# Attention and two mixing layers on one core: the last 64 tokens of q and k in one bank, and another rule for when the weights' parts are moved

## The chip, the cores and the metric

The kernel runs on one core of a Trainium2 chip. The metric is device time in microseconds of one execution, from the launch to the last output in memory. Below, block names and times refer to the profiled execution of the kernel before unless it is said otherwise.

## The reference

Three stages in fp32. The first is attention with exponential features, the second a gated channel mix, the third a convolution with a gate. Cut to what is computed:

```python
# q, k, v: (8, 8, 576, 64); w_phi: (64, 128)
proj = einsum('bhsd,df->bhsf', x, w_phi)
proj = proj - max(abs(proj), axis=-1)
phi(x) = concat([exp(proj), exp(-proj)])          # 256 features
kv = phi(k)^T v ; z = sum(phi(k)) ; out = phi(q) kv / (phi(q) z + 1e-6)
# channel mix on (8, 576, 512): xk, xr are mixtures of x and x one token back
k = relu(xk @ w_k) ; r = sigmoid(xr @ w_r) ; x2 = r * (k*k @ w_v)
# conv stage
h = relu(x2 @ w_in) ; out = (h * sigmoid(conv3(h, conv_w))) @ w_out
```

## The kernel before

**Attention.** Two heads of a batch are a pair; there are 32 pairs, and block(Pi) does the work around pair Pi. The 576 tokens are four tiles of 128 and a rest of 64. Tile `rqk` holds both heads of a pair: head h has the partitions 64h to 64h+63 (its 64 dimensions), and the columns are q of the first 512 tokens, then the last 64 tokens of q, then the last 64 of k, then the first 512 of k. A block runs on three pairs at once: it transposes the features of q of pair Pi (`turn`, `turn_end`: tiles `pt`, `pr`, features `qf` on ScalarE), projects the rest of q and k and the k of pair Pi + 2 (`front`: `rows_last` into `p1`, which the trace calls `p`, and `rows4` into `pk`), projects q of pair Pi + 1 (`pq`), sums kv of Pi + 1 (`pkv`), and computes the results of pair Pi (`pn`). VectorE centres each projection (`centre`: a reduction `mx` and a subtraction into `t`) and normalises the results (`rd`, `xn`); ScalarE makes the features of k (`kp` and, for the last 64 tokens, `kr`). The finished rows `xn` are transposed by `column` (`px`) and copied to `xT`.

**The last 64 tokens.** `rows_last` multiplies the 128 columns (64 of q, 64 of k) of each head with w_phi: two matmuls on 64 rows of the array, one for each head, each into a bank of its own. The tokens come out as partitions, 0 to 63 those of q, 64 to 127 those of k. `features` reads the k half for `kr` (four instructions on 64 partitions), `turn_end` transposes the q half, one transpose for each head.

**The channel mix.** u counts 16 half batches of 288 tokens. A u has 8 steps `psk`, and twice two steps `psr` and two `psv` (which take two credits each). Where one batch's four pairs are through, its u can run. `feed` gives steps behind block(Pi): none up to block 3, then 6, 6, 7 and 9 for blocks 4 to 7 (`SR`), 10 from block 8 on. u = 0 multiplies fp32 weights (`wkl`, `wrh`, `wvl`) directly, two instructions a matmul; later u use a high and a low half (three matmuls).

**The weights' parts.** w_k, w_r and w_v come as 64-bit floats and are turned into fp32 on the chip, 20 parts of 512 columns: 1 to 8 of w_k, 9 and 10 of w_r, 11 to 14 of w_v, 15 and 16 of w_r, 17 to 20 of w_v. `step` is a generator for one part with three stretches: SP loads `raw` (512 KB, three buffers); ScalarE reads it into `h`; VectorE finishes `h` with four instructions and SP stores it as a part (256 KB) into the weight tile. `tick()` sends one load off and finishes the part whose load went off two ticks earlier; `pre()` does ScalarE's read ahead of that tick. So the load of part k + 3, which needs the buffer of part k, stands on SP's queue behind the store of part k. Who calls tick: block(Pi) twice in blocks −1 to 6; `extras` at numbered places behind blocks 4, 5 and 6 (`WAT`); and `want(n)`, called by every step of a u with the number n of the part that it needs: it ticks until n + 2 parts (`AHEAD`) are done.

**What sets the order.** TensorE's instructions stand in the order in which the code above issues them, block by block, with the steps of the channel mix between blocks. For the other engines a scheduler orders the instructions at build time; on the chip each engine then takes its own in that order. `psm` is a ring of three PSUM banks (`p`, `pq` and the channel mix), `psa` one of five; from block 5 on a block takes from `psa` in turn `px`, `pt`, `pt`, `pr`, `pk`, `pk`, `pq`, `pkv`, `pn`, `pn`, so that the second `pk` takes the bank of `px`, the first `pq` that of the first `pt`.

Of the kernel before, what the change touches and what calls it, by code (L numbers as in the profile page):

```python
# [27 lines left out]

MS, SLOW, SR = 4, 8, {4: 6, 5: 6, 6: 7, 7: 9}

WAT = {4: (4, 10), 5: (3, 7, 11), 6: (3, 5, 7, 9)}
DS0 = 10
AHEAD = 2
HS = S // 2
V1 = D + 1

# [6 lines left out]
def fused_kernel(ctx: ExitStack, tc: tile.TileContext, qk, va, wphi, ones2, mu, wk, wv, wr, win, wout, cw, out):  # L43
# [113 lines left out]
    with ExitStack() as p1:  # L157
# [103 lines left out]
                T.matmul(o, x[r, j * P:j * P + P], wp0[r, h * FT:h * FT + FT], start=True, stop=True)  # L261

        def rows_last(Pi):
            ps = [psm.tile([P, 512], F32, tag="mm", name="p1") for _ in range(2)]
            ps = [p_[:, :FT].rearrange("p (a n) -> p a n", a=1) for p_ in ps]
            rows(Pi, [(ps[h][:, 0], h, 4) for h in range(2)])
            t = pool.tile([P, 1, 2, FT], F32, tag="t1", bufs=2, name="t")
            for h in range(2):
                centre(ps[h], t[:, :, h])
            ts[Pi] = [t]  # L270

        def rows4(Pi, j0, nm):
# [22 lines left out]
        def features(Pi, tk):  # L295
            kp = kps_[Pi] = []
            for h in range(2):
                k_ = pool.tile([P, 4, 2, FT], F32, tag="kp", bufs=2, name="kp")
                A.activation(k_[:, :, 0], tk[h], AF.Exp)
                A.activation(k_[:, :, 1], tk[h], AF.Exp, scale=-1.0)  # L300
                kp.append(k_)

            k_ = pool.tile([P, 2, FT], F32, tag="kr", bufs=1, name="kr")
            for h in range(2):
                r = slice(64 * h, 64 * h + 64)
                A.activation(k_[r, 0], ts[Pi][0][64:, 0, h], AF.Exp)
                A.activation(k_[r, 1], ts[Pi][0][64:, 0, h], AF.Exp, scale=-1.0)
            kp.append(k_)

        def sums4(Pi):  # L310
# [42 lines left out]
            return qf, t1  # L353

        def turn_end(qf, t1, pr):
            for h in range(2):
                T.transpose(pr[:, P + h * P:2 * P + h * P], t1[:, 0, h], ident)
            for h in range(2):
                for c in range(2):
                    A.activation(qf[h][:, c, 512:], pr[:, P + h * P:P + h * P + 64], AF.Exp, scale=1.0 - 2 * c)  # L360

        def results(Pi, qf):

# [24 lines left out]
        def block(Pi):  # L388

            nq, nk = Pi + 1 < B * NP, Pi + 2 < B * NP  # L390
            if 0 <= Pi < B * NP - 3:
                load(Pi + 3)
            if Pi >= 0:
                if Pi > MS:
                    x = column(Pi - 1)
                qf, t1 = turn(Pi)
                pr = psa.tile([P, 512], F32, tag="at", name="pr")
                if Pi > MS:
                    copies = column_end(*x, pr)
                turn_end(qf, t1, pr)  # L400
                if Pi > MS:
                    copies()
            pre()
            if nk:
                tk = front(Pi + 2)
            if -1 <= Pi < 7:
                tick()
            if 1 <= Pi <= MS:
                x = column(Pi - 1)
                column_end(*x, psm.tile([P, 512], F32, tag="mm", name="pr"))()  # L410
            if nq:
                ts[Pi + 1] += centre4(rows4(Pi + 1, 0, "pq"), "tq")
                del xk[Pi + 1]
                sums4(Pi + 1)
            if Pi >= 0:
                results(Pi, qf)
            pre()
            if nk:
                features(Pi + 2, tk)
                if Pi + 2 > 1:  # L420
                    load_v(Pi + 2)
            if -1 <= Pi < 7:
                tick()

        def attention(Pi):
# [39 lines left out]

        done = [0]

        def want(n):

            while ready[0] < min(n + AHEAD, 20):  # L470
                tick()
            due[0] += 1

        due = [0]
        needs = [*range(1, 9), 9, 10, 12, 14, 15, 16, 18, 20]

        def moe(u):
            b, hf = divmod(u, 2)

            def mm(ps, wh, wl, xh, xl, first, last):  # L480
                if u:
                    mm3(ps, wh, wl, xh, xl, first, last)
                else:
                    T.matmul(ps, f(wl), xh, start=first, stop=last)

            def need(n):
                want(n)
                if u:
                    split(n)

            def soon():
                if u == 0 and due[0] < len(needs) and ready[0] < min(needs[due[0]] + AHEAD, 20):
                    pre()
            o = hf * HS
            for j in range(2):
                while not mix_next(u, j):
                    yield
            xh, xl = mixed.pop((u, 0))
            k2 = []
            for fp in range(FC // 2):  # L500
                kf = tmps.tile([P, 2, HS], F32, tag="tmp", name="kf")
                for j in range(2):
                    ps = psm.tile([P, 512], F32, tag="mm", name="psk")[:, :HS]
                    fc = 2 * fp + j
                    need(fc + 1)
                    for c in range(KC):
                        w = slice(fc * DM + c * P, fc * DM + c * P + P)
                        mm(ps, wkh[:, w], wkl[:, w], xh[:, c], xl[:, c], c == 0, c == KC - 1)
                    A.activation(kf[:, j], ps, AF.Relu)
                    soon()  # L510
                    if u == 1:
                        split()
                    yield
                if u == 0:
                    kh = main.tile([P, 2, HS], F32, tag="kh", bufs=4, name="kh")
                    A.square(kh, kf)
                    k2.append((kh, kh))
                    continue
                if u == 1:
                    A.square(kf, kf)  # L520
                else:
                    V.tensor_tensor(kf, kf, kf, ALU.mult)
                kh = main.tile([P, 2, HS], F32R, tag="kh", bufs=4, name="kh")
                kl = main.tile([P, 2, HS], F32R, tag="kl", bufs=4, name="kl")
                A.copy(kh, kf)
                V.tensor_tensor(kl, kf, f(kh), ALU.subtract)
                k2.append((kh, kl))
            rh, rl = mixed.pop((u, 1))
            for mp in range(2):
                sg = main.tile([P, 2, HS], F32, tag="sg", bufs=1, name="sg")  # L530
                for j in range(2):
                    ps = psm.tile([P, 512], F32, tag="mm", name="psr")[:, :HS]
                    mc = 2 * mp + j
                    need(9 + 6 * mp + j)
                    for c in range(KC):
                        w = slice(mc * DM + c * P, mc * DM + c * P + P)
                        mm(ps, wrh[:, w], wrl[:, w], rh[:, c], rl[:, c], c == 0, c == KC - 1)
                    A.activation(sg[:, j], ps, AF.Tanh, scale=0.5)
                    soon()
                    if u == 1:  # L540
                        split()
                    yield
                mix_next(u + 1, mp)
                x2 = tmps.tile([P, 2, HS], F32, tag="tmp", name="x2")
                for j in range(2):
                    ps = psm.tile([P, 512], F32, tag="mm", name="psv")[:, :HS]
                    mc = 2 * mp + j
                    need(12 + 6 * mp + 2 * j)
                    for kc in range(FC):
                        w = slice(mc * DFF + kc * P, mc * DFF + kc * P + P)  # L550
                        kh, kl = k2[kc // 2]
                        mm(ps, wvh[:, w], wvl[:, w], kh[:, kc % 2], kl[:, kc % 2], kc == 0, kc == FC - 1)
                    if u < 2:
                        split()
                    soon()
                    yield
                    if u < 2:
                        split()
                    V.scalar_tensor_tensor(x2[:, j], sg[:, j], 1.0, ps, ALU.add, ALU.mult)
                    yield  # L560
                (SY if u else G).dma_start(x2s[b][:, 2 * mp:2 * mp + 2, o:o + HS], x2)
# [12 lines left out]
        load_v(1)  # L574

        def extras(Pi, n):
            if n in WAT.get(Pi, ()):
                tick()
            if n + 1 in WAT.get(Pi, ()):
                pre()  # L580
            if Pi == 7 and n == 14:
                taps()
            if Pi >= DS0 and dsteps and n in (3, 11):
                dsteps[0] = dsteps[0][0](), dsteps[0][1]
            if Pi >= DS0 and dsteps and n in (4, 12):
                raw, step = dsteps.pop(0)
                step(raw)
# [177 lines left out]
```

## Time and profile before

| | us |
|---|---|
| median of the runs (range) | 1225.81 (1225.13 to 1226.35) |
| the profiled execution | 1225.83 |
| its span, first to last instruction | 1224.0 |
| TensorE busy | 1202.0 (98%) |
| VectorE busy | 762.1 (62%) |
| ScalarE busy | 696.7 (57%) |

In the page's slices TensorE is at 7 to 8 tenths in the first two and at 9 from the third on, while VectorE begins at 7, 9, 8 and 9 tenths and falls to 5 to 7. The granted clock is full in every slice. Of the chain that ended last TensorE holds 90%. The busy share is thus high throughout, and what tells the two regimes apart is which wait of TensorE ends last in a given block.

### The profile page before, as it was taken

How to read it: one execution, taken by the hardware profiler on the slowest of the kernel's cores; microseconds unless marked ns; L12 is line 12 of the kernel's file. 1: busy time of each engine (PE TensorE's matmuls, PEld its weight loads, DVE VectorE, ACT ScalarE, POOL GpSimd, SP SyncE). 2: the span in 40 equal slices, each digit the busy share in tenths (PEclk: the TensorE clock that was granted, in tenths of full speed). 3: DMA queues.
4: the chain of work that ended last, by engine and by line, in shares of the span. 5: the costliest groups of instructions: out<-in, count | busy, mean ns of one | idle time of the engine just before them, and what ended most of it. 6: DMA issues, size and time to landing. Idle time of an engine off the chain costs nothing.

```text
span 1224.0 us, 29034 instructions
## 1 busy us (share of the span) xinstructions
PE 1202.0 (98%) x11920; PEld 1135.5 (93%) x11920; DVE 762.1 (62%) x1584; ACT 696.7 (57%) x1644; POOL 86.3 (7%) x213
## 2 busy tenths in 40 slices
PE   7899999999999999999999999999999999999998
PEld 6787999999999999999999999998889888888887
DVE  7989676576675765766656534426555754466555
ACT  6777765566565655665555533325654655455554
POOL 1000001111111111111000000000000000000000
PEclk9999999999999999999999999999999999999999
DMA  6665121223232322332110004050122101210220
GB/s 223 221 218 196 59 80 59 86 93 120 89 93 76 117 83 86 93 121 71 50 42 23 11 21 158 20 188 19 44 63 63 43 21 62 63 53 11 63 62 32
DMA packets 56532, 100.81 MB, mean 82 GB/s; under 512 B 10320, under 2 KB 38608, under 8 KB 56400
## 3 DMA queue, kind: packets, MB, share of 16 engines
q1 hardware_dynamic: 40272, 61.65, 14.8%
q0 software_dynamic: 6768, 27.69, 7.4%
q10 hardware_dynamic: 9360, 9.61, 2.8%
q8 instruction: 94, 1.54, 0.5%
q14 instruction: 38, 0.31, 0.1%
HBM read 66.42 MB, written 27.26 MB: 77 GB/s over the span
## 4 chain that ended last, share of the span: by engine, by line
PE 90%; DVE 5%; ACT 2%; issue 1%; DMA 1%; SPq 0%; ACTq 0%; DVEq 0%
PE psh L150 5%; PE psh L152 5%; PE psh L151 5%; PE psv L150 5%; PE pkv L318 5%; PE psv L151 5%; PE psk L151 5%; PE psv L152 5%; PE psk L152 5%; PE psk L150 5%; PE pso L150 5%; PE pso L151 5%; PE pso L152 5%; PE pn L371 4%; PE psr L150 3%; PE psr L151 3%
## 5 line engine op out<-in xcount | busy, mean ns | idle before, releaser
L58 DVE SCALAR_TENSOR_TENSOR ct<-h,cw,ct 128x460 f32<-128x460 f32 (+2 forms) x160 | 111.4, 696 | 84.6 <-ACT ct L58 83.5
L150 PE MATMUL psv<-kh,wvl 128*128 128x288 f32 x480 | 142.2, 297 | 0.0
L151 PE MATMUL psv<-kl,wvh 128*128 128x288 f32 x480 | 141.9, 296 | 0.0
L151 PE MATMUL psk<-ml,wkh 128*128 128x288 f32 x480 | 141.7, 295 | 0.0
L152 PE MATMUL psk<-mh,wkh 128*128 128x288 f32 x480 | 141.4, 295 | 0.0
L152 PE MATMUL psv<-kh,wvh 128*128 128x288 f32 x480 | 141.1, 294 | 0.0
L150 PE MATMUL psk<-mh,wkl 128*128 128x288 f32 x480 | 140.9, 294 | 0.0
L152 PE MATMUL psh<-xh,wih 128*128 128x462 f32 (+1 forms) x320 | 118.9, 372 | 0.0
L151 PE MATMUL psh<-xl,wih 128*128 128x462 f32 (+1 forms) x320 | 118.8, 372 | 0.0
L151 PE MATMUL pso<-gl,woh 128*128 128x460 f32 (+1 forms) x320 | 117.9, 370 | 0.0
L152 PE MATMUL pso<-gh,woh 128*128 128x460 f32 (+1 forms) x320 | 117.7, 370 | 0.0
L58 ACT ACTIVATE kf<-psk 128x288 f32<-128x288 f32 x128 | 52.2, 408 | 111.5 <-PE psk L152 105.6
L150 PE MATMUL psh<-xh,wil 128*128 128x462 f32 (+1 forms) x320 | 107.3, 372 | 0.0
L58 ACT ACTIVATE h<-psh 128x462 f32<-128x462 f32 (+3 forms) x128 | 47.8, 409 | 76.8 <-PE psh L152 75.6
L150 PEld LDWEIGHTS psv<-kh,wvl 128*128 128x128 f32 x480 | 90.3, 188 | 0.8
L151 PEld LDWEIGHTS psv<-kl,wvh 128*128 128x128 f32 x480 | 90.4, 188 | 0.0
L150 PEld LDWEIGHTS psk<-mh,wkl 128*128 128x128 f32 x480 | 90.2, 188 | 0.1
L151 PEld LDWEIGHTS psk<-ml,wkh 128*128 128x128 f32 x480 | 90.2, 188 | 0.0
L152 PEld LDWEIGHTS psv<-kh,wvh 128*128 128x128 f32 x480 | 90.2, 188 | 0.0
L152 PEld LDWEIGHTS psk<-mh,wkh 128*128 128x128 f32 x480 | 90.2, 188 | 0.0
L58 ACT ACTIVATE kp<-t 128x512 f32<-128x512 f32 x128 | 70.3, 618 | 34.6 <-PE pkv L318 28.9
L58 DVE SCALAR_TENSOR_TENSOR x<-sg,psv 128x288 f32<-128x288 f32 x64 | 29.0, 454 | 97.5 <-PE psv L152 91.4
(108 smaller groups left out, 2822.7 us busy)
## 6 DMA issues: line engine op xcount, KB each, us to landing
rqk<-qk POOLq DMA_DIRECT2D x29, 576.0 KB, 4.8
va<-va POOLq DMA_DIRECT2D x30, 325.0 KB, 4.8
x2s<-x SPq DMA_DIRECT2D x30, 288.0 KB, 2.3
raw<-wk SPq DMA_DIRECT2D x8, 512.0 KB, 5.4
raw<-wv SPq DMA_DIRECT2D x8, 512.0 KB, 4.0
raw<-win SPq DMA_DIRECT2D x16, 256.0 KB, 2.9
raw<-wout SPq DMA_DIRECT2D x16, 256.0 KB, 2.9
x2r<-x2s ACTq DMA_DIRECT2D x16, 231.0 KB, 2.6
```

What stands on the lines that cost most here:

```text
L58: x = op(*a, **k)
L150: T.matmul(ps, wl, xh, start=first, stop=False)
L151: T.matmul(ps, wh, xl, start=False, stop=False)
L152: T.matmul(ps, wh, xh, start=False, stop=last)
L318: T.matmul(o[r:r + 64], k_[:, r:r + 64], v_, start=(i == 0), stop=(i == len(prods) - 1))
L371: T.matmul(pn[b_][64 * r:64 * r + 64, j], qf[h_][:, c, o:o + 64], kv[:, c, h_], start=(j == 0 and c == 0), stop=(j == 4 - b_ and c == 1))
```

## The change

**The last 64 tokens.** `rows_last` takes one bank instead of two. Four matmuls, one for each head and each of q and k, use 64 rows by 64 columns of the array: a head's rows and the partitions of the same head at the output. q and k lie side by side in the bank, [128 partitions, 2, 128], where the partitions are 64 tokens of each head. One reduction and one subtraction centre all of it; `kr` is made by two instructions on 128 partitions; `turn_end` has one transpose for both heads.

**The parts.** `WAT` and `AHEAD` go. A block ticks once in blocks −1 to 4, a second time in −1 and 4 alone, and not in 5 and 6. The rest is left to the steps of u = 0: `needs` lists for every step the number of steps before it (a `psv` counts two) and the part it needs, and `goal()` is that part or 6 + 0.85 (at + 1), whichever is more, at most 20. Before a step, `want()` ticks until so many parts are done.

```diff
-WAT = {4: (4, 10), 5: (3, 7, 11), 6: (3, 5, 7, 9)}
+PRE, RATE = 6, 0.85
-AHEAD = 2
...
         def rows_last(Pi):
-            ps = [psm.tile([P, 512], F32, tag="mm", name="p1") for _ in range(2)]
-            ps = [p_[:, :FT].rearrange("p (a n) -> p a n", a=1) for p_ in ps]
-            rows(Pi, [(ps[h][:, 0], h, 4) for h in range(2)])
-            t = pool.tile([P, 1, 2, FT], F32, tag="t1", bufs=2, name="t")
-            for h in range(2):
-                centre(ps[h], t[:, :, h])
+            x = xk[Pi]
+            ps = psm.tile([P, 512], F32, tag="mm", name="p1")[:, :2 * FT].rearrange("p (a n) -> p a n", a=2)
+            for a in range(2):
+                for h in range(2):
+                    r = slice(D * h, D * h + D)
+                    T.matmul(ps[r, a], x[r, 512 + D * a:512 + D * a + D], wp0[r, h * FT:h * FT + FT], start=True, stop=True)
+            t = pool.tile([P, 2, FT], F32, tag="t1", bufs=2, name="t")
+            centre(ps, t)
             ts[Pi] = [t]
...
-            for h in range(2):
-                r = slice(64 * h, 64 * h + 64)
-                A.activation(k_[r, 0], ts[Pi][0][64:, 0, h], AF.Exp)
-                A.activation(k_[r, 1], ts[Pi][0][64:, 0, h], AF.Exp, scale=-1.0)
+            A.activation(k_[:, 0], ts[Pi][0][:, 1], AF.Exp)
+            A.activation(k_[:, 1], ts[Pi][0][:, 1], AF.Exp, scale=-1.0)
...
-            for h in range(2):
-                T.transpose(pr[:, P + h * P:2 * P + h * P], t1[:, 0, h], ident)
+            T.transpose(pr[:, P:2 * P], t1[:, 0], ident)
...
             if nk:
                 tk = front(Pi + 2)
-            if -1 <= Pi < 7:
+            if -1 <= Pi <= MS:
                 tick()
...
-            if -1 <= Pi < 7:
+            if Pi in (-1, MS):
                 tick()
...
-        def want(n):
+        needs = [*zip([*range(11), 12, 14, 15, 16, 18], [*range(1, 11), 12, 14, 15, 16, 18, 20])]
+
+        def goal():
+            at, n = needs[0]
+            return min(20, max(n, int(PRE + RATE * (at + 1))))
 
-            while ready[0] < min(n + AHEAD, 20):
+        def want():
+            while ready[0] < goal():
                 tick()
-            due[0] += 1
+            needs.pop(0)
...
             def need(n):
-                want(n)
                 if u:
                     split(n)
+                else:
+                    want()
...
         def extras(Pi, n):
-            if n in WAT.get(Pi, ()):
-                tick()
-            if n + 1 in WAT.get(Pi, ()):
-                pre()
```

Three places show what this moves. On TensorE, the middle of block 5, from the transposes of the q features to the first projections of k. Before:

```order
L350 MATMUL pt<-ident,t 128x128 x8
L335 MATMUL pr<-ident,xn 128x128
L357 MATMUL pr<-ident,t 128x128 x2
L261 MATMUL p_1366<-wp_74,rqk 128x128
L261 MATMUL p_1367<-wp_74,rqk 128x128
L261 MATMUL pk<-wp_74,rqk 128x128 x8
```

After:

```order
L349 MATMUL pt<-ident,t 128x128 x8
L334 MATMUL pr<-ident,xn 128x128
L355 MATMUL pr<-ident,t 128x128
L268 MATMUL p_1323<-wp_74,rqk 64x128 x4
L260 MATMUL pk<-wp_74,rqk 128x128 x8
```

One of the two transposes of the last tokens is gone, and the two matmuls into two banks have become four into one bank; the rest stands as it was.

On VectorE, the start of block 2, from the results of the block before to the centring of `pk`; `h<-h` and `h<-raw,h` are the instructions of a tick, `p_` with a number is the tile of the last 64 tokens. Before:

```order
L58 TENSOR_SCALAR xn<-pn,rd 128x128
L58 TENSOR_SCALAR h<-h 128x512
L58 TENSOR_REDUCE mx<-p_676 128x1
L58 TENSOR_REDUCE mx<-p_677 128x1
L58 TENSOR_SCALAR h<-h 128x512
L58 TENSOR_TENSOR t<-p_676,mx 128x128
L58 TENSOR_TENSOR t<-p_677,mx 128x128
L58 SCALAR_TENSOR_TENSOR h<-raw,h 128x512
L58 TENSOR_REDUCE mx<-pk 128x4 x2
L58 SCALAR_TENSOR_TENSOR h<-raw,h 128x512
L58 TENSOR_TENSOR t<-pk,mx 128x512 x2
```

After:

```order
L57 TENSOR_SCALAR xn<-pn,rd 128x128
L57 TENSOR_REDUCE mx<-p_639 128x2
L57 TENSOR_TENSOR t<-p_639,mx 128x256
L57 TENSOR_REDUCE mx<-pk 128x4 x2
L57 TENSOR_TENSOR t<-pk,mx 128x512 x2
L57 TENSOR_SCALAR h<-h 128x512
```

The tick that stood ahead of and between the reductions of `pk` is no longer there; the block's other tick, which begins with the last row, stays.

On ScalarE, from the third step behind block 4 to the features of q in block 5; `h<-raw` is the read of a part, `kf` and `kh` belong to the steps of u = 0. Before:

```order
L58 ACTIVATE kf<-psk 128x288
L58 ACTIVATE h<-raw 128x512
L58 ACTIVATE kf<-psk 128x288
L58 ACTIVATE kh<-kf 128x576
L58 ACTIVATE kf<-psk 128x288 x2
L58 COPY xT<-px 128x512
L58 ACTIVATE kh<-kf 128x576
L58 ACTIVATE qf<-pt 128x512 x4
```

After:

```order
L57 ACTIVATE kf<-psk 128x288
L57 ACTIVATE h<-raw 128x512
L57 ACTIVATE kf<-psk 128x288
L57 ACTIVATE kh<-kf 128x576
L57 ACTIVATE kf<-psk 128x288
L57 ACTIVATE h<-raw 128x512
L57 ACTIVATE kf<-psk 128x288
L57 ACTIVATE h<-raw 128x512
L57 COPY xT<-px 128x512
L57 ACTIVATE kh<-kf 128x576
L57 ACTIVATE qf<-pt 128x512 x4
```

Two reads more stand between the last `kf` of the stretch and the features of q, the second of them, that of part 11, right ahead of the copy that frees the bank of `px`.

## Rows read from the trace of the kernel before

**Rows 1.** Stretches: window, us, busy (count) of PE PEld DVE ACT POOL, clock, DMA, GB/s.

```profile
400.00:425.00 25.00, 25.00 (x337) 24.64 (x334) 18.47 (x45) 15.24 (x41) 4.14 (x8) 1.00 0.34 105
```

**Rows 2.** Waits of PE: who waits, for whom: total us, times, longest.

```profile
PE pk L261 <- DVE xn L58: 4.9, 4, 1.2
...
PE pt L350 <- DVE t L58: 3.4, 5, 0.9
...
PE psv L484 <- DVE x L58: 0.7, 1, 0.7
PE pq L261 <- ACT qf L58: 0.7, 1, 0.7
PE pn L371 <- DVE t L58: 0.7, 1, 0.7
PE pk L261 <- ACT xT L58: 0.4, 1, 0.4
```

**Rows 3.** PE's timeline in a settled block: start, busy us, operation, count.

```profile
420.35 0.38 PE L357 MATMUL pr<-ident,t 128*128 128x128 f32 x2
420.66 0.49 PE L261 MATMUL p<-wp,rqk 64*128 64x128 f32 x4
420.98 1.06 PE L261 MATMUL pk<-wp,rqk 64*128 64x128 f32 x16
421.88 1.06 PE L261 MATMUL pq<-wp,rqk 64*128 64x128 f32 x16
422.87 2.09 PE L318 MATMUL pkv<-va,kp 128*64 128x65 f32 x64
424.78 0.61 PE L318 MATMUL pkv<-va,kr 128*64 128x130 f32 x8
```

**Rows 4.** PE's timeline from block 4 to block 7; brackets: the wait before.

```profile
62.01 1.25 PE L261 MATMUL pk<-wp,rqk 64*128 64x128 f32 x16 [1.23 <-DVE xn L58]
...
69.53 11.91 PE L484 MATMUL psk<-mh,wkl 128*128 128x288 f32 x48
...
83.33 1.06 PE L261 MATMUL pk<-wp,rqk 64*128 64x128 f32 x16
...
110.89 4.15 PE L484 MATMUL psv<-kh,wvl 128*128 128x288 f32 x16
...
127.49 0.60 PE L330 MATMUL px<-ident,xn 128*128 128x128 f32 x4
```

**Rows 5.** VectorE's timeline, block 0 and the blocks before 4.

```profile
21.16 0.43 DVE L58 TENSOR_SCALAR h<-h 128x512 f32<-128x512 f32 x1 [0.51 <-ACT h L58]
...
52.41 1.29 DVE L58 TENSOR_REDUCE mx<-pk 128x4 f32<-128x512 f32 x2
53.61 0.69 DVE L58 SCALAR_TENSOR_TENSOR h<-raw,h 128x512 uint32<-128x512 uint32 x1
...
64.09 1.29 DVE L58 TENSOR_REDUCE mx<-pk 128x4 f32<-128x512 f32 x2
```

**Rows 6.** VectorE's timeline, a tick that stands alone.

```profile
115.93 0.88 DVE L58 TENSOR_SCALAR h<-h 128x512 f32<-128x512 f32 x2
116.85 1.42 DVE L58 SCALAR_TENSOR_TENSOR h<-raw,h 128x512 uint32<-128x512 uint32 x2
```

**Rows 7.** ScalarE's timeline around block 5.

```profile
77.05 0.68 ACT L58 ACTIVATE h<-raw 128x512 f32<-128x512 f32 x1 [0.97 <-DMA raw<-wv]
...
81.91 0.59 ACT L58 COPY xT<-px 128x512 f32<-128x512 f32 x1
...
82.98 2.05 ACT L58 ACTIVATE qf<-pt 128x512 f32<-128x512 f32 x4
```

**Rows 8.** DMA issues, 66 to 82 us: count, KB each, median us to landing.

```profile
raw<-wv SPq DMA_DIRECT2D x4, 512.0 KB, 4.6
```

**Rows 9.** DMA issues, 91 to 107 us.

```profile
raw<-wv SPq DMA_DIRECT2D x3, 512.0 KB, 3.7
wvl<-h SPq DMA_DIRECT2D x2, 256.0 KB, 2.3
```

More of the change, by code (lines that the diff above doesn't have):

```diff
@@ L355, in turn_end @@
         def turn_end(qf, t1, pr):
-            for h in range(2):
-                T.transpose(pr[:, P + h * P:2 * P + h * P], t1[:, 0, h], ident)
+            T.transpose(pr[:, P:2 * P], t1[:, 0], ident)
             for h in range(2):
                 for c in range(2):
-                    A.activation(qf[h][:, c, 512:], pr[:, P + h * P:P + h * P + 64], AF.Exp, scale=1.0 - 2 * c)
+                    A.activation(qf[h][:, c, 512:], pr[:, P + h * D:P + h * D + D], AF.Exp, scale=1.0 - 2 * c)
         def results(Pi, qf):
@@ L466, in fused_kernel @@
         done = [0]
-        def want(n):
-            while ready[0] < min(n + AHEAD, 20):
+        needs = [*zip([*range(11), 12, 14, 15, 16, 18], [*range(1, 11), 12, 14, 15, 16, 18, 20])]
[4 more added lines that the diff above has]
+            while ready[0] < goal():
                 tick()
-            due[0] += 1
-        due = [0]
-        needs = [*range(1, 9), 9, 10, 12, 14, 15, 16, 18, 20]
+            needs.pop(0)
         def moe(u):
@@ L486, in need @@
             def need(n):
-                want(n)
                 if u:
                     split(n)
+                else:
+                    want()
             def soon():
-                if u == 0 and due[0] < len(needs) and ready[0] < min(needs[due[0]] + AHEAD, 20):
+                if u == 0 and needs and ready[0] < goal():
                     pre()
```

## The prediction

> **What bounds the kernel now.** I read the table of stretches first. In a settled stretch TensorE is busy for all of 25.00 us at a granted clock of 1.00, VectorE for 18.47 and ScalarE for 15.24 [rows 1]: from block 7 on, whatever TensorE does per block is time. Then the waits of TensorE: what repeats is 4.9 us in four waits of `pk` for VectorE's `xn` (1.2 each) and 3.4 in five of `pt` for its `t`; then there are single ones of 0.7 us: `psv` for `x`, `pq` for `qf`, `pn` for `t` [rows 2]. They lie in the first 120 us. There the timeline shows the other regime: `pk` of block 4 starts at 62.01 after a wait of 1.23 [rows 4], and VectorE's `mx<-pk` come at 52.41 and 64.09 [rows 5], a period of 11.68 us that VectorE sets. TensorE takes over with the first `psk` at 69.53 [rows 4]. So the change is judged in two places: the price of the quarters on TensorE in each settled block, and when the parts of the weights come while u=0 runs (69.53 to 127.49, where block 7's `px` starts [rows 4]).
>
> **Quarters, per settled block.** Before, from the first transpose of `t1` to `pk` it is 420.98 − 420.35 = 0.63 us [rows 3]. An instruction of 288 columns takes 11.91 / 48 = 0.248 (`psk`, [rows 4]), so one of 128 columns 0.11, and one on half of the rows goes beside its partner: the 16 of `pk` take 421.88 − 420.98 = 0.90, that is 8 × 0.11 [rows 3]. The 0.63 are thus two transposes (0.22), two pairs of `p` (0.22) and 0.19 left over: `p` starts 0.31 after two transposes worth 0.22, and `pk` 0.32 after two pairs worth 0.22. I read these as the price of changing from the whole array to halves. Another change, from `pq` to `pkv`, shows the same: 422.87 − 421.88 = 0.99 where `pk` to `pq` is 0.90, +0.09 [rows 3].
> After: one transpose 0.11; `p` is four matmuls of two instructions, where the q and the k of a head share a quarter, so only the two heads go together: 4 × 0.11 = 0.44; the 0.19 stay; and quarters to halves is one more change, +0.10 to +0.15. Sum 0.84 to 0.89, against 0.63: **+0.25 per block**.
> The Trainium skill, "TensorEngine Tiling (Array Packing)", section "Key Properties", says that a change of the tiling mode drains the array; the 0.09 and 0.10 above agree, and by it the further change costs about as much again, as in my sum.
> Bounds: if only one change is paid in all, 0.11 + 0.10 + 0.44 = 0.65, and 0.03 for the first load: +0.05. A gain is excluded, since the two matmuls of a head lie on the same quarter. At the other end no pair overlaps, since both heads now write one bank: +0.44 more, 0.69.
> It counts in blocks 5 to 29 (`p` belongs to pair Pi + 2): 25 blocks, of which I take two off, since 5 and 6 wait anyway (below). Blocks 30 and 31 lose a transpose, −0.2. 23 × 0.25 − 0.2 = **+5.5**; ends +1.0 and +15.7. ScalarE's and VectorE's savings (two `kr` for four, one centre for two) are hidden there: neither is full [rows 1].
>
> **Blocks 0 to 3, with one tick.** Before, a block holds two ticks, after it one from block 0 on. The tick that falls away is two `h<-h` and two `h<-raw,h`; alone it takes 116.85 − 115.93 = 0.92 and then some 1.33 of the 1.42 [rows 6], 2.25 in all; between other work somewhat less. VectorE is the bound, so this is no cover but period. From `mx<-pk` at 52.41 to the next `pk` at 62.01 it is 9.60, in which one `h<-raw,h` of the tick taken away also lies, at 53.61; an operation of 128x512 steps at 0.60 (53.61 − 52.41 for two) [rows 5]. The other three stand between `pk` and `mx<-pk`: 64.09 − 62.01 = 2.08, most of it theirs. Without them `mx<-pk` waits only for `pk` itself, 1.25 [rows 4] and about 0.03 behind it, with 0.05 for the quarters: 9.00 + 1.33 = 10.3 is the period after. 1.33 less, three times, is 4.0. In block 0 a wait of 0.51 for ScalarE [rows 5] goes, since `kr` halves. **−4.5**; `psk` starts near 65.0. TensorE, which waits 1.2 at `pk` and up to 0.9 at `pt` in such a block [rows 2], is late next; its waits shrink by the 1.33 and the quarters and do not quite go.
>
> **Block 5, with eleven parts asked for.** The price of fewer early ticks: 5 parts stand at the end of block 4 where there were 9, and the rule asks for 11 before block 5 is through. Each needs a buffer of three: the load of part k + 3 goes out on SP's queue right behind the store of part k. A load takes 4.6 at its median there and 3.7 later [rows 8, 9], ScalarE's read 0.68 [rows 7], VectorE's four 2.25 [rows 6], the issue of store and load about 0.6: a round of 7.2 to 8.1, three parts at a time. `pk` of block 4 now starts at 62.01 − 4.5 = 57.5; VectorE's work from there to the end of part 5 sums to some 9.0, so load 8 goes out at 67.2, its part is stored near 74.6, load 11 goes out at 75.2 and lands at 79.0 to 80.4. ScalarE is in order, and its read of part 11 stands ahead of `xT<-px`, `kh` and the four `qf`. The read (0.68) and the copy (0.5 to 0.59 [rows 7]) done, `px`'s bank is free for the second `pk` at 80.2 to 81.6; TensorE would be there at 83.33 − 4.5 + 0.2 = 79.0 [rows 4], and `kh` and two `qf` (0.51 each, 2.05 / 4 [rows 7]) hold up `pq` by some 0.5 more than now. **+2.5** (1.7 to 3.2). Before, these reads stood behind `qf`, so only what was loaded long ago was waited for: the waits there, 0.4 and 0.7, are in [rows 2].
>
> **Block 6.** Load 16 goes out behind tick 13, 9.95 into the round after block 5, and its read stands between `xT<-px` and `qf`. 3.7 to 4.4 for the load, 0.68, a `wkh` cast like the copy of `xT` (0.5) and two `qf` (1.0) add up to 15.8 to 16.5 after the block before, where TensorE comes to `pq` at some 14.85: it is held for **+1.3** (1.0 to 1.65). The wait of `pn` for `t` (0.65) goes, since VectorE has fewer ticks between: −0.65.
>
> **Parts 17 to 20.** They were done with the earlier ticks; now tick 16 stands behind `xn` of block 6 and 17 to 20 follow in turn. Tick 16 ends 4.0 after the block (1.7 for `rd` and `xn`, 2.25), tick 17 at 7.6; load 20 goes out 0.65 later and takes 4.4 (12.65), the read 0.7 (13.35), VectorE's instructions with those between 3 to 4, the store 2.3 [rows 9], and the second half of the last `psv` after that, 2.0 (half of its 16 instructions, 4.15 [rows 4]): block 7 starts 20.75 to 21.75 after block 6. Before it was 127.49 − 110.89 = 16.6 [rows 4], 0.70 of waiting in it. **+4.65** (4.15 to 5.15).
> Sum of the early part: −4.5 + 2.5 + 1.3 − 0.65 + 4.65 = **+3.3** (−1 to +5.5).
>
> **Sum.** The profiled execution took 1225.83 (span 1224.0), the median of the runs is 1225.81, so nothing is to be converted: 1225.8 + 3.3 + 5.5 = **1234.6**.
>
> **Rivals.** (A) *The further change is free:* TensorE counts quarters and halves as one mode, or hides the change behind the weight load. For it: the 0.19 may be two first loads. Against: 0.09 where `pq` goes to `pkv`. 1225.8 + 3.3 + 1.0 = 1230.1.
> (B) *The other side, the parts come in time:* if load 11 lands before 76.7, that is within 1.5 us, or if loads need not wait for their round because VectorE finishes part 8 some 3 us earlier than I put it, then neither block 5 nor 6 waits and parts 17 to 20 run behind matmuls. Then the gain of the early blocks stays: −4.5 − 0.65 − 0.70 = −5.85, with my quarters 1225.5 and with the free change 1221.0. For it: TensorE had nearly no wait in this stretch before [rows 2]. Against: with three buffers and 7.2 at the least per round, the reads now stand ahead of the transposes' copies.
> (C) *Two heads in one bank go one after the other:* 1225.8 + 3.3 + 15.7 = 1244.8. Against: `pkv` and `pn` have pairs in one bank, and the 64 instructions of `pkv` (65 columns, 0.056 each) take 424.78 − 422.87 = 1.91, two at a time [rows 3]; those pairs differ in columns, not in rows. For it: all pairs that differ in rows (`p`, `pk`, `pq`) have two banks now. The Trainium skill, "TensorEngine Tiling (Array Packing)", section "Gotcha 1: PSUM Pressure", says that different row tiles cannot reach the same bank at once. No row shows such a pair before; hence a chance of its own.
> (D) *The change doesn't do what it says:* the single bank frees `psm` sooner, but no wait in the settled stretch is for a bank [rows 1], so there is nothing to gain: inside the forecast.
>
> **How the numbers follow.** Forecast 0.45 (own range 1230 to 1239, by the early part's ends and 0.84 to 0.89 for the quarters). A 0.20, B 0.25, C 0.10. About 0.2% (1223.4 to 1228.3) is what a measurement of this kernel can tell from no change. Faster takes B with cheap quarters, 0.15; the same takes B with mine (0.10) and A with a good early part (0.07); the rest is slower, 0.68. The range leaves out C and the best of B: 1224 to 1241, where the upper end lets a fifth of C come on top of the forecast's own range.
>
> **What would show it.** Right: `pr` to `pk` near 0.88 in a settled block; `psk` first at 65.0; `pk` of block 5 held by ScalarE for some 2 us, with ScalarE waiting for the load of part 11; block 7's `px` near 130.8. Wrong: 0.68 there (A) or over 1.2 (C); block 7 before 125 (B).

## The result, and the profile after

The changed kernel takes 1240.06 us (median; 1239.14 to 1241.16) against 1225.49 of the kernel before in the same session: ratio 1.0116, 95% interval 1.0101 to 1.0132. It is 14.6 us slower, where 8.8 were forecast. The profiled execution, the fastest of the four, took 1239.14; its span is 1237.4, 13.4 more than the span before. The account below goes by these 13.4.

TensorE's waits in the whole span, changed kernel (who waits, for whom: total us, times, longest):

```profile
PE psv L486 <- DMA wvl<-h: 4.3, 4, 1.7
PE pk L260 <- DVE xn L57: 3.6, 4, 1.0
PE pk L260 <- ACT xT L57: 2.4, 2, 2.2
PE pq L260 <- ACT qf L57: 1.1, 2, 0.7
```

Against [rows 2] the waits of `pt` for `t` are gone and those of `pk` for `xn` are shorter; in their place stand waits of `psv` for the stored parts and of `pk` for the copy of `xT`. TensorE's timeline from block 4 to block 7 of the changed kernel, to be laid beside [rows 4]:

```profile
57.58 1.25 PE L260 MATMUL pk<-wp,rqk 64*128 64x128 f32 x16 [0.91 <-DVE xn L57]
...
65.11 11.91 PE L486 MATMUL psk<-mh,wkl 128*128 128x288 f32 x48
...
79.06 0.48 PE L260 MATMUL pk<-wp,rqk 64*128 64x128 f32 x2
81.76 1.77 PE L260 MATMUL pk<-wp,rqk 64*128 64x128 f32 x14 [2.22 <-ACT xT L57]
83.32 2.08 PE L260 MATMUL pq<-wp,rqk 64*128 64x128 f32 x16
85.33 2.17 PE L317 MATMUL pkv<-va,kp 128*64 128x65 f32 x64
...
89.97 4.15 PE L486 MATMUL psk<-mh,wkl 128*128 128x288 f32 x16
...
111.38 4.15 PE L486 MATMUL psv<-kh,wvl 128*128 128x288 f32 x16
...
132.80 0.60 PE L329 MATMUL px<-ident,xn 128*128 128x128 f32 x4
```

`psk` starts 4.4 us earlier than before; by 89.97 the lead is gone (89.78 before), and block 7 starts at 132.80 where it was 127.49: 5.31 late. The rest of the 13.4 is in the settled blocks. The starts of `pt` tell it block by block, in us and as the difference to the kernel before; the other columns are the experiments of the next section:

| block | before | changed | ticks_only | quarters_only | after_ml_behind | four_quarters |
|---|---|---|---|---|---|---|
| 4 | 58.88 | −3.99 | −4.51 | −0.39 | −4.44 | +0.60 |
| 5 | 81.71 | −4.42 | −4.93 | −0.38 | −4.91 | +0.60 |
| 6 | 101.96 | +0.19 | −2.18 | −0.13 | −0.16 | +0.75 |
| 7 | 127.92 | +5.32 | +3.92 | −0.34 | +4.63 | +0.80 |
| 12 | 248.08 | +6.35 | +3.92 | +0.69 | +5.67 | +1.39 |
| 13 | 272.54 | +7.02 | +3.93 | +1.36 | +5.92 | +2.19 |
| 14 | 297.02 | +7.29 | +3.92 | +1.62 | +6.19 | +2.33 |
| 26 | 590.66 | +12.73 | +3.92 | +7.10 | +9.31 | +7.76 |
| 31 | 712.89 | +13.36 | +3.93 | +7.73 | +9.94 | +8.14 |

From block 7 on the changed kernel loses 8.0 us in two sorts of blocks: +0.26 in most (none in blocks 8 and 26), and from block 12 to block 25 every second one 0.61 to 0.68. A part of the differences stands already at the start: the first transposes of block 0 come 0.44 later than before in the changed kernel, 0.74 earlier in `ticks_only`, 0.41 later in `quarters_only` and 0.30 earlier in `after_ml_behind`.

### The profile page after: what moved, and what is told of

Its sections match the earlier page's. It is cut to its first block, busy times and chain, and to the rows that moved or that the text cites. A ratio compares the mean times of both kernels' runs of the same rounds, so it can differ in the third digit from the quotient of the medians.

```text
span 1237.4 us, 29080 instructions
## 1 busy us (share of the span) xinstructions
PE 1214.4 (98%) x12016; PEld 1140.6 (92%) x12016; DVE 763.1 (62%) x1520; ACT 675.6 (55%) x1580; POOL 86.3 (7%) x213
## 4 chain that ended last, share of the span: by engine, by line
PE 79%; DVE 11%; issue 4%; ACT 3%; DMA 2%; POOL 1%; SPq 0%; ACTq 0%; POOLq 0%; DVEq 0%
PE psv L149 5%; PE psh L149 5%; PE psh L151 5%; PE psh L150 5%; PE psv L150 5%; PE psv L151 5%; PE pso L149 5%; PE pso L150 5%; PE pso L151 5%; PE pkv L317 4%; PE psk L150 4%; PE psk L151 4%; PE psk L149 4%; PE pn L369 3%; DVE mx L57 2%
```

## The experiments

**Each part alone.** "The quarters" are the new way for the last 64 tokens, after the four quarters of the array. `ticks_only` is the changed kernel with the old `rows_last`, `features` and `turn_end`; `quarters_only` is the kernel before with the new ones.

> The changed kernel with the last 64 tokens done as before (two matmuls into two banks, two centrings, four kr instructions, two transposes): only the rule for the parts is new. Theory: the rule alone moves the first psk ahead by about 4 us and then loses 9 to 10 us in blocks 5 to 7, since loads that take three buffers round are waited for; block 7's transposes come 4.5 to 5.5 us later than in the kernel before, and from there on the two run alike, 24.47 us a block. Time about 1230 to 1231. Rival (the quarters bring on the early loss, through the order of ScalarE's work): block 7 no later than before, 1225 to 1227.

Measured 1232.77 (1229.77 to 1234.38), ratio 1.0054 (1.0038 to 1.0069); the profiled execution was the fastest. Block 7 is 3.92 late and stays so to the end. Both miss the expectation a little, the median above 1230 to 1231 and the lateness below 4.5 to 5.5. The waits in it are those of the changed kernel, without the quarters (TensorE's timeline):

```profile
80.39 1.16 PE L260 MATMUL pk<-wp,rqk 64*128 64x128 f32 x14 [1.62 <-ACT xT L57]
81.95 1.16 PE L260 MATMUL pq<-wp,rqk 64*128 64x128 f32 x16 [0.40 <-ACT qf L57]
...
103.47 1.16 PE L260 MATMUL pq<-wp,rqk 64*128 64x128 f32 x16 [1.01 <-ACT qf L57]
...
119.31 2.18 PE L487 MATMUL psv<-kh,wvl 128*128 128x288 f32 x8 [1.72 <-DMA wvl<-h]
```

So the rule for the parts makes the early loss by itself; the rival falls.

> The kernel before with the new way for the last 64 tokens; the rule for the parts as before. Theory: each settled block costs +0.26 us for the change of the array's geometry and the doubled work (25 blocks, 6.4), and in every second block from 12 to 25 another 0.4 us (7 times, 2.7), since VectorE's order now has the subtraction ml<-xf between the two last subtractions of pq, which hold a bank that the first psv wants. Early part between -1 and 0. Time 1233 to 1235. Rival (the extra 0.4 comes from the rule for the parts): 1230 to 1232, every settled block +0.26 alike.

Measured 1233.46 (1232.89 to 1233.58), ratio 1.0061 (1.0044 to 1.0078). The early part is as before (−0.34 at block 7), and both sorts of blocks are there: the quarters, and not the rule for the parts, bring the 0.4 in every second block. The two parts alone make +7.0 and +7.7 against their session's 1225.77, 14.7 together, against 14.6: the medians add up. The profiled spans do so less well: 4.0 and 7.8 make 11.8 of 13.4.

**The 0.4 us in every second block.** Block 18 to 19 of the changed kernel and of the kernel before are alike, but for +0.26 up to `pkv`, until the step from `psr` to `psv`. The changed kernel, TensorE and VectorE (timelines):

```profile
415.47 0.29 PE L151 MATMUL psr<-mh,wrh 128*128 128x288 f32 x1
415.87 0.37 PE L149 MATMUL psv<-kh,wvl 128*128 128x288 f32 x1
```

```profile
413.77 0.69 DVE L57 TENSOR_TENSOR t<-pq,mx 128x512 f32<-128x512 f32 x1
414.37 0.76 DVE L57 TENSOR_TENSOR ml<-xf,mh 128x576 fp32r<-128x576 f32 x1
415.04 0.69 DVE L57 TENSOR_TENSOR t<-pq,mx 128x512 f32<-128x512 f32 x1
```

The kernel before at the same place, TensorE and VectorE:

```profile
406.11 0.29 PE L152 MATMUL psr<-mh,wrh 128*128 128x288 f32 x1
406.25 0.29 PE L150 MATMUL psv<-kh,wvl 128*128 128x288 f32 x1
```

```profile
404.69 1.29 DVE L58 TENSOR_TENSOR t<-pq,mx 128x512 f32<-128x512 f32 x2
405.88 0.17 DVE L58 TENSOR_SCALAR rd<-pn 128x5 f32<-128x5 f32 x1
405.95 0.76 DVE L58 TENSOR_TENSOR ml<-xf,mh 128x576 fp32r<-128x576 f32 x1
```

In the changed kernel `ml<-xf` stands between the two last subtractions of `pq`. The bank of the second `pq` comes free at 415.04 + 0.69 = 415.73, and this `psv` takes that bank of the ring of three; it starts at 415.87, 0.40 behind the last `psr` where it was 0.14 (0.26 more), and loses another 0.1 while it picks up. The profile puts no name to so short a wait. The order comes from the build; why it lets `ml` ahead here is not shown. `kr` takes half its time on ScalarE, which could make `mh` ready earlier in the scheduler's reckoning, but `four_quarters` (below) has the same order with ScalarE's work as it was. `after_ml_behind` adds one rule to the changed kernel:

```diff
+            last_c[0] = V.tensor_tensor(t, ps, mx..., ALU.subtract).ins        # in centre
...
+                tc.add_manual_dep(x_.ins, last_c[0].name, ...)                 # x_ is ml<-xf
```

> The changed kernel with one added rule of order on VectorE: ml<-xf stands behind the last subtraction of a projection that was issued before it, so that both subtractions of pq come together again as in the kernel before. Nothing else. Theory (the bank held by the late subtraction is the 0.4 us in every second block): the settled blocks become alike, 24.73 us each, and the time falls by 2.5 to 3 us against the changed kernel, to about 1237.3. Rival (the 0.4 us comes from elsewhere, a DMA or the array): 1240, with the two lengths of block still alternating.

Measured 1236.57 (1235.73 to 1237.49), 3.5 less than the changed kernel (another session; 2.5 to 3 were expected). The two subtractions stand together again (VectorE's timeline):

```profile
411.89 1.29 DVE L57 TENSOR_TENSOR t<-pq,mx 128x512 f32<-128x512 f32 x2
413.09 0.76 DVE L57 TENSOR_TENSOR ml<-xf,mh 128x576 fp32r<-128x576 f32 x1
```

The blocks from 12 to 25 are now alike, each 0.25 to 0.27 longer than before, and from block 7 to 31 the difference grows by 5.3 instead of 8.0: 2.7 less. The theory holds. Of the 3.4 between the two profiled spans the other 0.7 stand at the transposes of block 0 already, ahead of all that the rule moves.

**Geometry or doubled work.** `four_quarters` is the kernel before with its two matmuls of 64x128 each cut in two of 64x64, on four different quarters, two banks as before.

```diff
-            rows(Pi, [(ps[h][:, 0], h, 4) for h in range(2)])
+            x = xk[Pi]
+            for a in range(2):
+                for h in range(2):
+                    r, o_ = slice(D * h, D * h + D), slice(D * a, D * a + D)
+                    T.matmul(ps[h][o_, 0], x[r, 512 + D * a:512 + D * a + D], wp0[r, h * FT:h * FT + FT], ...)
```

> The kernel before in which each of the two matmuls of the last 64 tokens is cut in two of 64 rows by 64 columns, the four on four different quarters of the array, in two banks, results at the same places as before. All else as before. It measures the price of one more geometry without the doubled work on one quarter. If a change of geometry costs 0.10 to 0.15 us wherever it happens: from the start of p to pq +0.10 to +0.15 in every settled block, 1228.5 to 1230. If the changed kernel's +0.25 is the doubled work alone: +0, 1225.5 to 1226. If four quarters don't run at once: +0.25 or more, 1232.

Measured 1233.40 (1232.80 to 1234.51), ratio 1.0063 (1.0048 to 1.0078), far over what was expected. TensorE's timeline of a settled block of this kernel, and under it the changed kernel's:

```profile
449.87 0.38 PE L361 MATMUL pr<-ident,t 128*128 128x128 f32 x2
450.18 0.45 PE L270 MATMUL p<-wp,rqk 64*64 64x128 f32 x8
450.56 1.16 PE L261 MATMUL pk<-wp,rqk 64*128 64x128 f32 x16
451.55 1.06 PE L261 MATMUL pq<-wp,rqk 64*128 64x128 f32 x16
```

```profile
430.12 0.27 PE L355 MATMUL pr<-ident,t 128*128 128x128 f32 x1
430.32 0.65 PE L268 MATMUL p<-wp,rqk 64*64 64x128 f32 x8
430.90 1.16 PE L260 MATMUL pk<-wp,rqk 64*128 64x128 f32 x16
431.90 1.06 PE L260 MATMUL pq<-wp,rqk 64*128 64x128 f32 x16
```

From `pr` to `pq` it is 1.68 in this kernel, 1.78 in the changed one and 421.88 − 420.35 = 1.53 before [rows 3]. The finer cut, with the further change of geometry in it, costs 0.15 with no column more for any quarter, within what was expected; whether the change itself or the eight smaller instructions with their weight loads make the 0.15, the run does not tell apart. The doubled work (0.22) less the transpose (0.11) is the other 0.10 of the changed kernel. The changed kernel's eight instructions take 0.58 to `pk`; one after the other they would take 8 × 0.11 = 0.88, in pairs 0.44. So the two heads do run together into one bank. Most of the rest of the 8.1 in the table is put down to the order again: in this kernel too `ml<-xf` has come between the two subtractions (409.49, between 408.89 and 410.16), and every second block from 12 to 25 costs 0.73 to 0.80 instead of 0.15. No run took the order back here. That VectorE's order would move in a kernel whose VectorE work is unchanged was not expected.

**When the parts are asked for.** Four kernels with the old way for the last tokens: `t_pre4` asks for 4 + 0.85 (at + 1) parts instead of 6 + 0.85 (at + 1); `t_56` keeps the second tick in blocks 5 and 6; `t_pre4_56` does both; `before_one_tick` is the kernel before without the second tick in blocks 0 to 3. The lines of the first two are given against the changed kernel, the last against the kernel before.

```diff
-PRE, RATE = 6, 0.85
+PRE, RATE = 4, 0.85                                # t_pre4
...
-            if Pi in (-1, MS):
+            if Pi in (-1, MS, MS + 1, MS + 2):     # t_56
...
-            if -1 <= Pi < 7:
+            if -1 <= Pi < 7 and not 0 <= Pi < MS:  # before_one_tick
```

> The run ticks_only with 4 + 0.85 (at + 1) parts asked for instead of 6: by block 5 nine are asked for, not eleven, and the read of the last one ahead of the copy of px is of a part loaded some 2.5 to 5 us earlier. Theory (block 5 is held by the load of part 11, block 6 by the load of part 16 standing ahead of qf, the rest by parts 17 to 20 coming late): the waits of pk and pq in block 5 (2.0 us) and of pq in block 6 (1.0) go, block 6 begins near 97.5, and part of that is given back in front of block 7, since six loads then stand behind block 6 instead of four: block 7 at 129.5 to 132, time 1227.5 to 1231. Rival (block 5 waits for something else, VectorE's order or the centring of p): block 6 at 99.8 as in ticks_only.

> The run ticks_only with the second tick of a block kept in blocks 5 and 6 too. Theory: block 5 waits as in ticks_only (its reads stand the same), but two more parts are asked for before block 6 ends, so that psv waits for the last parts (5.2 us in ticks_only) fall to 2 to 3: block 7 at 128.5 to 130.5, time 1226.5 to 1229. Rival (the round of three buffers is full from block 5 on, so that ticks asked for earlier only wait longer): block 7 at 131 to 133.

> The kernel before without the second tick in blocks 0 to 3, and nothing else changed: its ticks behind blocks 4 to 6 and its rule of two parts ahead stay. It has the gain of the early blocks (first psk about 4 us earlier) with a slower demand in block 5 (eight parts, not eleven). Theory (the early loss is the demand outrunning the loads, not the parts moved to later blocks): block 5 waits at most 1 us, block 7 at 124 to 127.5, time 1222.5 to 1226. Rival (whatever parts are not done by block 4 are paid later, since VectorE and the three buffers have no room in blocks 5 to 7): block 7 at 129 or later, 1227 or more.

> Both: nine parts asked for by block 5, and the second tick of a block kept in blocks 5 and 6. Theory: no wait in block 5 and shorter ones for the last parts, so that some of the early gain stays: block 7 at 126 to 128.5, time 1224 to 1227. Rival (the buffers' round): block 7 at 130 or later.

| kernel | median us | block 5 | block 6 | block 7 |
|---|---|---|---|---|
| before | 1225.72 | 81.71 | 101.96 | 127.92 |
| t_pre4 | 1252.40 | 77.67 | 105.35 | 155.86 |
| t_56 | 1231.75 | 77.65 | 101.92 | 134.92 |
| before_one_tick | 1233.96 | 77.30 | 104.11 | 135.33 |
| t_pre4_56 | 1253.02 | 77.03 | 105.21 | 157.16 |

All four have the 4 us of the early blocks, and all four lose more than that. Fewer parts asked for do take the wait of `pk` out of block 5 (0.4 in all for `xT` in `t_pre4`), as the theory had it, but the expectation of block 6 and 7 missed widely, in `t_pre4_56` too. `t_pre4` behind block 6, TensorE, then VectorE:

```profile
131.93 2.75 PE L487 MATMUL psv<-kh,wvl 128*128 128x288 f32 x8
139.81 3.90 PE L487 MATMUL psv<-kh,wvl 128*128 128x288 f32 x8 [5.13 <-DMA wvl<-h]
149.28 6.31 PE L487 MATMUL psv<-kh,wvl 128*128 128x288 f32 x16 [5.57 <-DMA wvl<-h]
```

```profile
143.75 0.46 DVE L57 SCALAR_TENSOR_TENSOR x<-sg,psv 128x288 f32<-128x288 f32 x1 [5.15 <-PE psv L487]
144.12 0.88 DVE L57 TENSOR_SCALAR h<-h 128x512 f32<-128x512 f32 x2
145.03 1.42 DVE L57 SCALAR_TENSOR_TENSOR h<-raw,h 128x512 uint32<-128x512 uint32 x2
```

VectorE's instructions for the next part stand behind `x`, which waits for the `psv` that waits for the part before. Matmuls, VectorE and the store then run one after the other instead of beside each other. A part of what these kernels lose is TensorE's clock, which drops after several of the waits: over the span the mean granted clock is 0.991 in `t_pre4` and 0.986 in `t_pre4_56`, against 1.000 before. `t_56` does not help either: block 5 waits 2.02, and the four `psv` 6.2 in all; its block 7 comes later than both its theory and its rival said. In `before_one_tick` block 5 hardly waits, and its steps pay: 5.3 for `wvl` and 2.8 for `wrh`. Its rival was right: a part that isn't done by block 4 costs more later than the second tick costs in blocks 0 to 3.

**A version that is faster than both.** Since parts cannot be put off, the tick was made cheaper for VectorE: `pool_max` is the kernel before with the first of its four instructions on GpSimd.

```diff
-            V.behind("tensor_scalar", h, h, 2.0 ** -31, 122879.9921875 * 2.0 ** -16, ALU.max, ALU.min)
-            V.tensor_scalar(hu, hu, 3, None, ALU.logical_shift_left)
+            G.tensor_scalar(h, h, 2.0 ** -31, 122879.9921875 * 2.0 ** -16, ALU.max, ALU.min)
+            V.behind("tensor_scalar", hu, hu, 3, None, ALU.logical_shift_left)
```

> The kernel before with the first of VectorE's four instructions of a part (the clamp of h between two constants) on GpSimd, which is idle for most of the span; the rest as before, two ticks a block. It follows from the runs before: parts put off are paid dearer later, so the tick should cost VectorE less instead of being put off. Theory (blocks 0 to 3 are as long as VectorE's work, an instruction of 128x512 counts 0.33 there): 0.66 less in each of four blocks, first psk 2.0 to 2.7 us earlier, nothing lost later since the same parts are asked for at the same places: 1223 to 1224. Rivals: GpSimd takes some 2.5 us for it (1.30 for half the size in the settled blocks), VectorE in its order waits for it, and the period stays or grows: 1226 to 1230; or VectorE's own instructions get longer beside GpSimd's: the mean of h<-raw,h above 0.70.

Measured 1226.17 (1225.41 to 1226.60), ratio 1.0001 (0.9991 to 1.0011). That is what the first rival said. Blocks 2 and 3 are 0.45 shorter (11.23 and 11.21 against 11.68), but block 0 is 11.30 long against 8.58: VectorE waits there for the first part.

```profile
22.92 0.43 DVE L58 TENSOR_SCALAR h<-h 128x512 uint32<-128x512 uint32 x1 [2.84 <-POOL h L58]
```

> pool_max with the clamp of the very first part back on VectorE. In pool_max VectorE stood still for 2.84 us at that place in block 0, waiting for GpSimd, while the blocks after it were 11.2 to 11.5 us long instead of 11.7, so that block 7 began at the same time as before. Theory: block 0 is as long as in the kernel before, the gain of the others stays: block 7's transposes 2 to 2.7 us earlier than in the kernel before, time 1223.2 to 1224. Rival (the next part then waits for GpSimd in block 1 in its place): 1225.5 to 1226.5.

Measured 1227.71 (1226.48 to 1227.88), ratio 1.0015 (1.0006 to 1.0024), more than theory and rival said. Without `behind` the first part's clamp had moved ahead of the centring of `pk`, and the wait only changed its name:

```profile
21.25 0.43 DVE L58 TENSOR_SCALAR h<-h 128x512 f32<-128x512 f32 x1 [3.11 <-ACT h L58]
```

> pool_max2 with the clamp of the first part held behind VectorE's work of the blocks before it, as in the kernel before. In pool_max2 it stood ahead of the centring of pk in block 0, and VectorE waited there 3.11 us for ScalarE's read; from block 3 on its blocks were 11.2 us long and block 4's 22.18 against 22.83. Theory: block 0 and 1 as in the kernel before, 0.45 less in blocks 2 and 3 each, 0.65 in block 4, 0.3 in block 6: block 7's transposes 1.8 to 2.4 us ahead of the kernel before, 1223.3 to 1224. Rival (a wait for GpSimd takes the gain in another place): 1225.5 or more.

Measured 1224.32 (1223.65 to 1224.80) against 1225.63 in its session, ratio 0.9988 (0.9979 to 0.9997); 1223.3 to 1224 were expected. Block 0 is 8.57 long, block 7 starts 2.22 earlier than in the kernel before. It beats both kernels, the kernel before by only 0.12%, but its slowest execution is faster than the fastest of the other (1225.01); of the 2.2 between the profiled spans 1.3 show in the medians.

## Why the forecast was right in direction and short in size

The range (1224 to 1241) holds the 1240.06, and slower was the likeliest. That it holds it is luck: the forecast's own range ended at 1239, and the room above was left for rival C, which did not come. Of the 13.4 us between the spans the forecast had 8.8. Step by step:

**Blocks 0 to 3: right.** −4.5 forecast, 65.11 − 69.53 = −4.4 measured (−4.9 when the later start of block 0 is taken out); the period was put at 10.3 and is 10.2 (44.66 to 54.89 between two `pt`).

**Block 5: mechanism right, a term missing.** ScalarE's order and the round of loads were as forecast. SP's queue and ScalarE in the changed kernel:

```profile
67.07 0.54 SPq L173 DMA_DIRECT2D raw<-wk  x1
...
75.01 0.54 SPq L173 DMA_DIRECT2D raw<-wv  x1
```

```profile
80.57 0.67 ACT L57 ACTIVATE h<-raw 128x512 f32<-128x512 f32 x1 [0.94 <-DVE h L57]
81.15 0.56 ACT L57 COPY xT<-px 128x512 f32<-128x512 f32 x1
```

Loads 8 and 11 go out at 67.07 and 75.01 (forecast 67.2 and 75.2), load 11 lands 5.5 after its issue, near 80.5 (forecast 79.0 to 80.4), and the read starts at 80.57; the wait is put down to VectorE's `h`, but the load is what came last. `pk` waits 2.22 for the copy. What the forecast put at nothing is what follows the wait: TensorE's granted clock falls to half. The changed kernel in stretches, columns as in [rows 1]:

```profile
81.70:83.40 1.70, 1.64 (x16) 1.55 (x16) 1.67 (x6) 1.70 (x5) 0.00 (x0) 0.63 0.46 177
83.40:85.40 2.00, 2.00 (x19) 1.77 (x20) 2.00 (x5) 1.96 (x9) 0.00 (x0) 0.50 0.94 271
85.40:87.40 2.00, 2.00 (x66) 2.00 (x68) 2.00 (x5) 0.34 (x2) 0.53 (x1) 0.97 0.94 271
```

At 0.50, which is 1.2 GHz, the last 14 instructions of `pk` take 1.56 where 0.79 is due, `pq` 2.01 where it is 0.99, `pkv` 2.00 where it is 1.91: 1.9 us. The clock is 1.7 of it, counting what it lacks of 1.00 in each stretch: 0.37 × 1.70 + 0.50 × 2.00 + 0.03 × 2.00. The other 0.2 a start behind a wait costs at full clock too: in `ticks_only` (1.00) the 14 of `pk` behind the wait are busy for 1.16, where 16 without a wait are for 1.06 [rows 3]. Block 5 costs 4.6 in all (89.97 − 65.11 = 24.86 against 89.78 − 69.53 = 20.25): 2.22, 1.9, 0.25 for the quarters, which the forecast had left out of this block, and some 0.2; the forecast term was 2.5.

**Block 6 and parts 17 to 20: right in kind, block 6 at half its size.** `pq` waits 0.65, below the forecast 1.0 to 1.65, and the wait of `pn` is gone as forecast; the block costs +0.3 (forecast 1.3 − 0.65). From block 6's end to block 7 it is 132.80 − 111.38 = 21.42 (forecast 20.75 to 21.75), +4.8 against the +4.65 forecast. Sum of the early part 5.3 instead of 3.3. By this trace the 1.9 behind the wait of block 5 are the difference; the other misses cancel. `ticks_only`, which kept its clock, fits this only in part: its block 5 costs 23.01 − 20.25 = 2.8, close to the forecast, but its way from block 6 to block 7 is 22.29, 0.9 longer than in the changed kernel. Most of that is one store: the last `psv` starts 3.11 after the issue of the store it needs, in the changed kernel 2.36. One store that lands later thus moves a term of this stretch by some 0.8.

**Quarters: right in size.** 0.26 per block where 0.25 was forecast, 5.3 in sum against 5.5. What it is made of is near the forecast too: 0.15 for the finer cut alone, and pairs that run together. It does not lie where the forecast put it, though: `pr` to `pk` is 430.90 − 430.12 = 0.78, halfway between its sign (0.88) and that of rival A (0.68); the other 0.10 comes behind, `pk` to `pq` taking 1.00 instead of 0.90. That sign alone would have decided nothing. Of the rivals, A falls with `four_quarters`, and C with the 0.58 us for eight instructions. The rule of the Trainium skill, "TensorEngine Tiling (Array Packing)", section "Gotcha 1: PSUM Pressure", by which different row tiles cannot reach one bank at once, did not hold for quarters that differ in rows and columns and so write different partitions of the bank; the measurement decides. Two row halves that write the same partitions of one bank were not tried.

**The order on VectorE: missing.** The forecast put the new way's effect on ScalarE and VectorE at nothing, since neither is full. That was the step that failed: the savings are hidden, but with the quarters the build gives VectorE another order, and a bank of `psm` comes free later. It costs 2.7 us, as `after_ml_behind` shows by taking it back. Rival D, too, had only asked for waits for a bank that were there before. It could have been seen in the order of the changed kernel, in which the subtractions of `pq` are split in every second block from 12 on; the forecast's working on VectorE's order ends with block 6.

3.3 + 5.5 was the forecast; 5.3 + 5.3 and 2.7 for the order make the 13.4, to a tenth. Block 7's `px` came at 132.80, 2.0 behind the 130.8 that was given as its sign. Rival B's point was missed far: load 11 would have had to land by 76.7 and came at 80.5, and `t_pre4` shows that to ask for less does not help.

What stays open: the medians of `ticks_only` spread over 4.6 us, and those of the changed kernel over 2. The profiled execution of `ticks_only` was its fastest and kept a granted clock of 1.000; two of the other three have a mean of 0.998 over the span, which points to a drop, but where was not traced. So the share of the clock in the medians is open, as is the 1.2 by which the 14.6 of the medians exceed the 13.4 of the traces. Why the build moved VectorE's order is open too.

## What to carry to other kernels

After any edit, compare the whole order of all engines after the build, not only the blocks that the edit names, and engines whose work is unchanged too: an instruction that has moved ahead can hold a buffer that the bound engine wants. Work that is put off from a phase that another engine bounds must have a phase that can hide it, with the length of its round through the buffers counted; asked for just in time it turns into a chain of load, compute, store and matmul in which nothing overlaps. And a wait of TensorE of some 2 us is to be priced with what its clock may then cost, here 1.7 us behind a wait of 2.22.

## What the runs showed of the hardware

Waits of TensorE of 2.22 us (changed kernel) and 2.02 (`t_56`) in the middle of dense work were followed by a granted clock of 0.50; one of 1.62 and, 1.2 us later, one of 0.40 in `ticks_only` were not (1.00 throughout). The length of the wait alone does not decide it: in `after_ml_behind` waits of 1.79 and then 0.40 were followed by 0.52 (82.45 to 84.45), while one of 1.81 before 121.50 in `t_56` was not, nor one of 2.58 before 97.37 in `t_pre4`, whose clock stood at 1.00 until a further wait of 1.93 at 101.48. The stretch of `t_56` right behind its wait:

```profile
81.60:83.40 1.80, 1.73 (x15) 1.73 (x17) 1.80 (x8) 1.80 (x5) 0.00 (x0) 0.50 0.60 226
```

Quarters on the diagonal run two at a time into one bank, 8 instructions of 128 columns in 0.58 us. On GpSimd the clamp of 128x512 takes 1.91 (`pool_max`, at 20.97), and one `h<-raw,h` of VectorE beside it took 1.13 instead of 0.68 (at 30.31, same run).
